# Coarser first loads, a reordered weight product and dummy matmuls at the start of an attention + SwiGLU kernel

## The chip, the cores and the metric

The kernel runs on one core of a Trainium2 chip. The metric is the device time of one execution in microseconds; most executions of one kernel agree within 0.3%. Engines: TensorE (PE, with its weight loads PEld), VectorE (DVE), ScalarE (ACT), GpSimd (POOL), SyncE (SP). L178 is line 178 of the kernel. The chain is the work that ended last, followed back from the last instruction: at each step to what released it. The granted clock is the share of TensorE's full clock that the records of a run show, as a mean over the span unless a time is given. A transfer lands when its completion is signalled.

## The reference, cut to what matters

```python
B, N, C = 4, 6016, 256;  d_ff = 1536;  tau = 1.0
qn = q / (norm(q, axis=1) + 1e-6);  kn = k / (norm(k, axis=1) + 1e-6)
s  = kn.transpose(0, 2, 1) @ qn / tau          # 256 x 256 per batch, summed over 6016 rows
a  = exp(s - s.max(-1));  a /= a.sum(-1) + 1e-9
x  = (v @ a).reshape(B * N, C)
out = (silu(x @ w_gate) * (x @ w_val)) @ w_out
```

The kernel folds the softmax into the weights: once a batch's 256 x 256 matrix is known, it multiplies it with `w_gate` and `w_val`, and the long stream of products with v begins. Batches 2 to 4 are prepared in the background of the one before; only batch 1 has to be read, squared, summed and normalized before anything else can run.

## The kernel before

The parts that the change and the argument touch; "..." marks cuts.

```python
groups = [(s, min(4, NS - s)) for s in range(0, NS, 4)]      # NS = 47 tiles of 128 rows
...
def gemm1_pair(b, t):      # L151, L156: products of q and k, two tiles at a time, into kq
def first_square(b, t, which, on_dve):                       # L165 VectorE, L168 ScalarE
    sq = sqpool.tile([P, 2, C], BF16, tag="sq%d" % which)     # 4 buffers
def first_row_sums(...):   # L178: sums of the squares over rows, by a product with ones
def first_cols / first_col_sums(...):                        # L191, L201: the same per column
...
def keep_warm(n):                                            # L382: results are never read
    ps = psum_o.tile([P, 2, C], FP32, tag="o")
    for _ in range(n):
        nc.tensor.matmul(ps, ones_bf, warm_bf, start=True, stop=True)
...
qgroups = groups[:-1] + [(s, min(2, NS - s)) for s in range(gs, NS, 2)]
order = [(g, 1, groups) for g in range(NG)] + [(g, 0, qgroups) for g in range(NQ)]
for n, (g, which, gl) in enumerate(order):
    load_qk(0, g, which, gl)           # float32 in HBM, fp8 in SBUF, issued by GpSimd
...
load_first_v(); load_w(0, HW); load_w(HW, WP); load_v(*allc[1])
for wc in range(1, NWC):
    load_w(wc * WP, (wc + 1) * WP)
...
for g, which, gl in order:
    ...
    sqs = [first_square(0, t, which, on_dve=(t % 2 == 1)) for t in ts]
    if which == 0:
        for t in ts: gemm1_pair(0, t)
        ...
    for t, sq in zip(ts, sqs):         # row sums of k; row, then column sums of q
        ...
    if which == 0:
        if g == 0: first_norm_k(0); ...
        elif g <= 4: first_inv_k(0, g - 1)      # a quarter of a reciprocal, L218
first_softmax(0)
```

## Time and profile before

| | |
|---|---|
| time, median of 3 | 813.78 us (813.57 to 814.0) |
| profiled span | 811.9 us |
| TensorE busy | 794.1 us |
| last q group landed | 34.07 us |
| first weight product (L392) | 36.53 us |
| TensorE waits for w_gate until | 40.55 us, and never again for long |

The prediction shows the lines and reads them.

### The profile page before, as it was taken

To read this page: it belongs to the slowest core of one execution; us is meant where nothing else is said; L and a number is where in the kernel's file an instruction comes from. 1 tells how busy PE (TensorE), PEld (TensorE's weight loads), DVE (VectorE), ACT (ScalarE), POOL (GpSimd) and SP (SyncE) were. 2 spreads that over 40 slices of the span, in tenths; PEclk is the share of its full clock that TensorE was granted. 3 is DMA by queue.
4 is the path that set the end of the run, shared out by engine and by line. 5 is a ranking of instruction groups with operands and counts; after the bars stand their busy time and mean duration, and the time that the engine had idled before them with its cause. 6 is when DMAs were issued, how large, how long until landed. Compare 5 with 4: busy or idle time off the path is not lost.

```text
span 811.9 us, 13668 instructions
## 1 busy us (share of the span) xinstructions
PE 794.1 (98%) x4952; PEld 488.9 (60%) x5042; DVE 524.3 (65%) x795; ACT 434.8 (54%) x757; POOL 267.2 (33%) x330
## 2 busy tenths in 40 slices
PE   5999999999999999999999999999999999999998
PEld 3656666665565666666565666666556565665666
DVE  4777777657556777656755677765765555555554
ACT  4666655545555556545555556654554544444543
POOL 5515887423000888722100488752300000000000
PEclk9999999999999999999999999999999999999999
DMA  9993875329312678334912377641942112112101
GB/s 87 142 157 69 115 105 86 80 34 150 77 40 46 96 100 106 74 65 95 127 40 59 53 96 112 89 78 37 171 102 66 46 50 55 52 40 65 50 27 59
DMA packets 93747, 64.99 MB, mean 80 GB/s; under 512 B 52896, under 2 KB 92448, under 8 KB 92928
## 3 DMA queue, kind: packets, MB, share of 16 engines
q0 software_dynamic: 19584, 27.41, 29.0%
q1 hardware_dynamic: 73952, 36.65, 18.2%
q8 instruction: 39, 0.64, 0.4%
q14 instruction: 28, 0.23, 0.1%
q10 hardware_dynamic: 144, 0.07, 0.0%
HBM read 79.04 MB, written 36.70 MB: 143 GB/s over the span
## 4 chain that ended last, share of the span: by engine, by line
PE 93%; DMA 4%; issue 1%; DVE 1%; POOL 0%; ACT 0%; POOLq 0%
PE o_new L457 30%; PE v_ps L423 30%; PE g_ps L423 28%; DMA q_sb<-in_q_dram 2%; PE ps L392 2%; PE kq_new L151 2%; DMA k_sb<-in_k_dram 1%; DMA w_gate_sb<-in_moe_w_gate_dram 1%; DVE sv L433 0%; POOL k_sb L106 0%; ACT silu L429 0%; PE last_ps L481 0%; POOL vb L114 0%; DVE sq L274 0%; PE kq_new L156 0%
## 5 line engine op out<-in xcount | busy, mean ns | idle before, releaser
L433 DVE TENSOR_TENSOR sv<-silu,v_ps 128x512 bf16<-128x512 bf16 (+1 forms) x576 | 388.3, 674 | 263.9 <-ACT silu L429 261.1
L429 ACT ACTIVATE silu<-g_ps 128x512 bf16<-128x512 f32 (+1 forms) x576 | 338.7, 588 | 323.4 <-PE g_ps L423 257.5
L457 PE MATMUL o_new<-w_out_sb,sv 128*128 128x256 bf16 x2244 | 337.2, 273 | 1.5
L423 PE MATMUL v_ps<-vT,Wv 128*128 128x512 bf16 (+1 forms) x1100 | 324.3, 374 | 2.9
L423 PE MATMUL g_ps<-vT,Wg 128*128 128x512 bf16 (+1 forms) x1074 | 319.1, 375 | 0.3
L457 PEld LDWEIGHTS <-sv 128*128 128x128 bf16 x2244 | 219.6, 98 | 140.6
L423 PEld LDWEIGHTS <-Wv 128*128 128x128 bf16 x1152 | 112.7, 98 | 130.7
L284 POOL TENSOR_TENSOR acc_new<-acc_new,sq 128x512 f32<-128x512 f32 x135 | 157.6, 1167 | 45.1 <-DVE sq L274 36.9
L423 PEld LDWEIGHTS <-Wg 128*128 128x128 bf16 x1152 | 109.7, 98 | 24.9
L274 DVE TENSOR_TENSOR sq<-q_sb 128x512 bf16<-128x512 fp8e5 x72 | 65.9, 915 | 0.0
L279 POOL TENSOR_TENSOR acc_new<-sq 128x512 f32<-128x512 bf16 x3 | 3.5, 1154 | 150.5 <-DVE sq L274 150.5
L275 ACT ACTIVATE sq<-k_sb 128x512 bf16<-128x512 fp8e5 x72 | 44.2, 614 | 0.0
L466 ACT COPY o_sb<-o_new 128x512 f32<-128x512 f32 x48 | 28.1, 586 | 14.9 <-PE o_new L457 14.5
L151 PE MATMUL kq_new<-k_sb,q_sb 128*128 128x512 fp8e5 x184 | 32.0, 295 | 0.5 <-DMA q_sb<-in_q_dram 0.5
L106 POOL DMA_DIRECT2D q_sb<-in_q_dram x49 | 27.4, 558 | 13.5 <-DMA k_sb<-in_k_dram 5.5
L468 DVE COPY o_sb<-o_new 128x512 f32<-128x512 f32 (+1 forms) x47 | 31.3, 666 | 0.0
L106 POOL DMA_DIRECT2D k_sb<-in_k_dram x48 | 26.0, 542 | 10.4 <-DMA w_out_sb<-in_moe_w_out_dram 5.6
L178 PE MATMUL ss_new<-sq,ones_bf 128*128 128x256 bf16 x83 | 17.8, 353 | 9.1 <-ACT sq L168 8.6
L114 POOL DMA_DIRECT2D vb<-in_v_dram x47 | 24.1, 515 | 5.3 <-DMA vb<-in_v_dram 4.1
L151 PEld LDWEIGHTS <-q_sb 128*128 128x256 fp8e5 x184 | 21.2, 138 | 2.6 <-DMA q_sb<-in_q_dram 2.0
L178 PEld LDWEIGHTS <-ones_bf 128*128 128x128 bf16 x83 | 9.9, 122 | 15.9 <-issue 11.6
L312 POOL TENSOR_TENSOR inv<-inv,half 128x4 f32<-128x4 f32 x3 | 3.1, 1036 | 36.7 <-DVE inv L311 36.7
(94 smaller groups left out, 195.9 us busy)
## 6 DMA issues: line engine op xcount, KB each, us to landing
out_dram<-o_sb SPq DMA_DIRECT2D x92, 256.0 KB, 2.5
vb<-in_v_dram POOLq DMA_DIRECT2D x43, 256.0 KB, 5.9
k_sb<-in_k_dram POOLq DMA_DIRECT2D x44, 128.0 KB, 5.9
q_sb<-in_q_dram POOLq DMA_DIRECT2D x44, 128.0 KB, 5.1
w_out_sb<-in_moe_w_out_dram POOLq DMA_DIRECT2D x1, 768.0 KB, 13.7
vb<-in_v_dram POOLq DMA_DIRECT2D x4, 192.0 KB, 3.5
vT<-vb SPq DMA_TRANSPOSE x47, 4.3
w_gate_sb<-in_moe_w_gate_dram POOLq DMA_DIRECT2D x2, 256.0 KB, 7.0
```

Source lines behind the costliest of these rows:

```text
L106: nc.gpsimd.dma_start(out=dst[:, gs:gs + gm, :], in_=src[b].rearrange("(p s) c -> p s c", s=NS)[:, gs:gs + gm, :])
L151: nc.tensor.matmul(kq[:, jh, :], q_sb[:, ps:ps + 2, js], k_sb[:, ps:ps + 2, :], start=(t == 0 and jh == 0), stop=last, perf_mode=DR, skip_ ...
L178: nc.tensor.matmul(state[b, "ss", which], ones_bf, sq[:, s, :], start=(t == 0 and s == 0), stop=(t == t_last and s == pm - 1))
L274: nc.vector.tensor_mul(sq[:, :pm, 0, :], q_sb[:, ps:ps + pm, :], q_sb[:, ps:ps + pm, :])
L275: nc.scalar.activation(sq[:, :pm, 1, :], k_sb[:, ps:ps + pm, :], ACT.Square)
L284: nc.gpsimd.tensor_tensor(out=acc, in0=acc, in1=sq[:, s, :, :], op=ALU.add)
L423: nc.tensor.matmul(dst[:, :mv], W[:, kk, fs], vT[:, kk, :mv], start=(kk == 0), stop=(kk == CH - 1))
L429: nc.scalar.activation(silu[:, :mv], g_ps[:, :mv], ACT.Silu)
L433: nc.vector.tensor_mul(sv[:, f, :mv], silu[:, :mv], v_ps[:, :mv])
L457: nc.tensor.matmul(self.o_ps[:, j % 2, :], self.sv[:, f, j * P:(j + 1) * P], w_out_sb[:, f, :], start=(f == 0), stop=(f == FH - 1))
L466: nc.scalar.copy(o_sb[:, :m, :], self.o_ps[:, :m, :])
L468: nc.vector.tensor_copy(o_sb[:, :m, :], self.o_ps[:, :m, :])
```

## The change

Its intent: fewer and larger transfers for batch 1's k and q (16 tiles each, then 8, 4, 2 and 1 for q, so that little is left to do after the last landing); a third weight product that needs only the first half of the exponentials; and dummy matmuls that keep TensorE busy while q is awaited. The diff, cut:

```diff
-        sq = sqpool.tile([P, 2, C], BF16, tag="sq%d" % which)
+        sq = sqpool.tile([P, 2, C], BF16, tag="sq%d" % which, bufs=8)
...
+        keep_warm(1)
         transpose_first_v()
-        keep_warm(3)
+        keep_warm(2)
...
         wp_matmul(b, 1, 0, units[1], lo)
+        wp_matmul(b, 2, 0, units[2], lo)
         row_sum(1)
         finish_rs(b, rs)
-        wp_matmul(b, 0, 1, units[0], lo)
-        wp_matmul(b, 1, 1, units[1], lo)
-        for u in (2, 3):
-            for jh in range(CH):
-                wp_matmul(b, u, jh, units[u], lo)
+        for u, jh in ((0, 1), (1, 1), (2, 1), (3, 0), (3, 1)):
+            wp_matmul(b, u, jh, units[u], lo)
...
+    kgroups = [(s, min(16, NS - s)) for s in range(0, NS, 16)]
+    qgroups, at = [], 0
+    while at < NS:
+        rest = NS - at
+        size = 16 if rest >= 39 else 8 if rest >= 23 else 4 if rest >= 4 else min(2, rest)
+        qgroups.append((at, size))
+        at += size
...
-            elif g <= 4:
-                first_inv_k(0, g - 1)
+            elif g <= 2:
+                first_inv_k(0, 2 * g - 2)
+                first_inv_k(0, 2 * g - 1)
+
+            if g < NQ - 2:
+                keep_warm(2)
```

In the changed kernel the dummies are L381, the weight products L391, the products with v L422.

## The prediction

> **What bounds the kernel now.** I read four views in this order: the page, the chain that ended last, the waits, and the timeline of the first 45 us. The page says that nearly the whole span is TensorE work; the chain says so too.
>
> ```profile
> span 811.9 us, 13668 instructions
> PE 93%; DMA 4%; issue 1%; DVE 1%; POOL 0%; ACT 0%; POOLq 0%
> ```
>
> The change touches only the first batch's start, so what it can be worth is read from the chain's early pieces (start, length, what):
>
> ```profile
> 22.93 10.19 DMA q_sb<-in_q_dram
> 33.12 0.28 issue
> 33.40 0.53 POOL vb L114
> 33.93 0.10 issue
> 34.03 6.52 DMA w_gate_sb<-in_moe_w_gate_dram
> 40.55 0.04 issue
> 40.60 1.04 PE ps L392 x4
> ```
>
> Up to 40.55 us the chain is one saturated stream of transfers (k, q, the first v, the weights); from 40.60 us TensorE runs without a gap to the end. So the time is 40.6 us of start plus some 771 us that this change leaves alone, and the change can win or lose only in how soon TensorE reaches that L392 product. The timeline tells what TensorE did before it (start, duration, engine, line, shapes; idle before in brackets):
>
> ```profile
> 7.36 1.01 PE L178 MATMUL ss_new<-sq,ones_bf 128*128 128x256 bf16 x4 [0.19 <-ACT sq L168]
> ...
> 24.74 0.60 PE L178 MATMUL ss_new<-sq,ones_bf 128*128 128x256 bf16 x4
> ...
> 25.24 0.65 PE L151 MATMUL kq_new<-k_sb,q_sb 128*128 128x512 fp8e5 x4
> 25.30 0.63 ACT L168 ACTIVATE sq<-q_sb 128x512 bf16<-128x512 fp8e5 x1 [0.61 <-DMA q_sb<-in_q_dram]
> 25.32 0.69 DVE L165 TENSOR_TENSOR sq<-q_sb 128x512 bf16<-128x512 fp8e5 x1
> ...
> 25.93 0.54 DVE L218 RECIPROCAL ink<-ink 128x64 f32<-128x64 f32 x1
> ...
> 34.82 0.38 PE L356 MATMUL rs<-eps,ones_f 1*128 1x2 f32 x2
> ...
> 36.53 0.38 PE L392 MATMUL unit_ps<-w_gate_sb,exT 128*128 128x256 bf16 x2
> ...
> 39.62 0.59 PE L423 MATMUL v_ps<-vT_new,Wv 128*128 128x512 bf16 x2
> 40.59 0.55 PEld L392 LDWEIGHTS <-exT 128*128 128x128 bf16 x4 [0.87 <-DMA w_gate_sb<-in_moe_w_gate_dram]
> ```
>
> The reader is to see three things. All engines keep pace with the loads: each group of four tiles is worked off as it lands, so that only about 0.8 us lies between the last q landing (34.07 us) and L356. From 36.53 us TensorE goes on without a pause until the issue of v_ps ends at about 40.05 us, then waits 0.55 us for the weights: that 0.55 us is all the room its own chain has. And the same four row-sum matmuls took 1.01 us at 7.36 us and 0.60 us at 24.74 us: start to start 213 ns then, 108 ns later, the step falling near 21.6 us.
>
> **What the Trainium skill says.** "DMA: Bandwidth & Descriptors", section "Why small descriptors are slow (HBM only)", gives a fixed cost of about 3 cycles per packet beside its 32-byte beats; with the 850 MHz of its section "Where 436 GB/s comes from", a 4096-byte read is (128+3)/0.85 = 154 ns. The trace agrees: the squares of the k groups start 1.25 us apart, and one engine moves 8 such packets a group, 1.233 us, which leaves 0.021 us for the completion. The packet records say that size is linear: 173 ns for 4096 source bytes, 98 for 2048, 60 for 1024, and 1226 for the 32768 of a v transfer, that is 37.65 ns per KB plus 22 ns, of which all but about 3.5 overlaps the next packet. "Perfetto Trace Analysis", section "DMA Optimizations", says that larger transfers amortize a per-transfer overhead but that splitting lets some work start sooner; this change trades the second for the first. "TensorE: Matmul & The Clock Gate", Part 1, says that the array runs at half rate until about 3.4 us of sustained work; the 213 and 108 ns agree, although the page's clock row shows 9 throughout.
>
> **The change part by part.**
>
> *Fewer transfers.* Per engine, k and q are now 25 transfers of 8 packets (200 packets, 25 completions); after, 3 + 8 = 11 transfers (88 packets, 11 completions). Saved: 112 x 3.5 ns + 14 x 21 ns = 0.69 us. Sixteen tiles take 8 x (16 x 37.65 + 3.5) + 21 ns = 4.87 us, fifteen 4.57, eight 2.46, four 1.25, two 0.65, one 0.35. The fourth k group landed at 9.22 us; less 24 packets and 3 completions (0.15) the first large one lands at 9.07, the next at 13.94 and 18.51, then q: 23.38 (16 tiles), 25.84, 28.30, 29.55, 30.80, 32.05, 32.70, 33.05. The stream is the same bytes at the same rate, so the large q group lands 3.2 us after the first small one did (20.18).
>
> *What the grouping moves.* No q work can begin before 23.4 us. From there TensorE works in program order: all products of a group, its row sums (column sums from the fifth group), two dummies of 0.216 us each for the first six groups. With the fast spacing, 0.109 us a product and 0.108 a row sum:
> - group 1: 23.4 + 16 x 0.109 = 25.14; 16 row sums 26.87; dummies 27.30.
> - group 2: 8 products 28.17. Its squares on VectorE come late: ScalarE has four squares and the two steps of ink first (23.4 + 4 x 0.63 + 0.79 = 26.71), VectorE the ink addition and a cast (27.2), two squares 28.60. Row sums 28.88, dummies 29.31. VectorE's two reciprocals (0.54 each): 29.68.
> - group 3: products 30.18; VectorE squares at 31.06; row sums 31.34; dummies 31.77; reciprocals 32.14.
> - group 4: products 32.21; square 32.83; row sums 33.11; dummies 33.54.
> - group 5: VectorE copies the row (0.41) at 33.33 and is at 33.74; the row's transposition on TensorE (0.54) ends at 34.52, column sums 34.74, dummies 35.17.
> - group 6: products 35.61, column sums 35.83, dummies 36.26.
> - groups 7 and 8: products 36.73, column sums 36.92; L356 is done at 37.17, against 35.07 now.
>
> The check on this sum: TensorE's q work after 23.4 us is 48 x 0.109 + 36 x 0.108 + 0.54 + about 0.6 for column sums = 10.3 us, plus 12 dummies x 0.216 = 2.6 us: 36.3 us even without one wait. VectorE alone has 11 x 0.69 + 0.42 + 0.5 + 4 x 0.54 + 0.41 = 11.1 us: 34.5 us.
>
> *The softmax.* Now the first exponentials end 1.48 us after the last column sum (34.755 to 36.23). After: 36.92 + 1.48 = 38.40, first weight product about 38.50 + 0.05. The dummy before the transposes fills a wait for v that is gone by then (v lands near 34.3); TensorE's own list would be through at 38.3, so it costs nothing.
>
> *The third product.* It puts one 0.108 us matmul ahead of the second row sum, which now starts at 36.75 with no gap before it; after, it fills part of the 0.45 us between the two exponentials. Worth 0 to 0.1 us; I leave a stall of 0.1 us.
>
> *Sum.* First weight product 38.55 + 0.10 against 36.53: 2.1 us later. Of this 0.55 us is the room before the weights; they land earlier themselves, so TensorE no longer waits for them. 2.1 - 0.55 = 1.55 us. 813.78 + 1.55 = 815.3 us.
>
> **Rivals.**
> 1. The transfers stay the bound. Then the whole start moves with them: -0.7 us, 813.1. For it: at present everything after 12 us waits on landings, and bigger packets may also help in the ragged first microsecond, where some packets took up to 1.08 us. Against it: even at zero overhead the large q group can't land much before 22.5 us, and the 13 us of TensorE work behind it then pass 35.4.
> 2. TensorE is slow when the large q group lands. TensorE idles for about 1 us before it. If it stays slow until 26.8 or 28.4 us (one or two windows of the size that the skill gives), the same addition ends 1.0 to 1.9 us later: 816.4 to 817.2. Against it: in bursts of sixteen row sums at 213 ns (3.4 us without pause of every 4.9 us) it has a better chance to warm up during k than now, where 0.85 us of every 1.25 never did. I go by warm.
> 3. The dummies do no harm, because TensorE waits for VectorE anyway. Taking them out of my addition moves the first weight product about 1 us earlier, not 2.6, so VectorE's backlog is the other half; 814.3 would be the result if they hid completely.
>
> **Range and chances.** All of this is a fraction of 1% of the span: nothing in 40 us of start can lose or gain the 16 us that 2% asks for. Rival 1 bounds the low side with rival 3 inside, rival 2 the high side. I take 813.9 to 817.2, with about one chance in ten that it comes out faster than now. Chances: faster by over 2% 0.005, within 2% 0.985, slower by over 2% 0.01.
>
> **What would show the steps right or wrong.** Landings: ScalarE's squares of k should resume near 9.1, 13.9 and 18.5 us, and of q near 23.4; if q's come before 22.5, the saving per packet is larger than I think. In the waits, q's squares should no longer be ended by the transfer from group 2 on, but run back to back on VectorE. L356 near 36.9 and the first L392 near 38.6; TensorE should not wait for w_gate at all, and the chain should run through L178, L151, VectorE's squares and the dummies' line in place of the transfer of w_gate. If L356 comes before 35 us, the backlog was misjudged and rival 1 holds; if the row sums after 23.4 us are 213 ns apart, rival 2 does.

## The result, and the profile after

| | before | after |
|---|---|---|
| time, median of 6 runs each | 813.83 us (813.57 to 814.0) | 815.17 us (814.92 to 815.57) |
| profiled span | 811.9 us | 813.2 us |
| w_gate's second columns landed | 40.55 us | 39.90 us |
| first weight product | 36.53 us | 38.26 us |
| first product with those columns | 40.60 us | 41.80 us |

The ratio is 1.0017 (95% interval 1.0004 to 1.003): 1.3 us slower. Ratios here are the mean time of one kernel's runs over that of the other's of the same rounds, so not quite the ratio of the medians.

The page of the changed kernel, the lines that answer to those of before:

```profile
span 813.2 us, 13666 instructions
PE 95%; DMA 2%; issue 1%; DVE 0%; ACT 0%; POOL 0%; POOLq 0%
```

DMA's share of the chain is halved. The chain itself (start, length, what) shows where it went:

```profile
3.59 19.71 DMA q_sb<-in_q_dram
23.31 0.04 issue
23.35 1.96 PE kq_new L151 x16
25.31 1.76 PE ss_new L178 x16
...
29.27 0.43 PE ps L381 x2
29.70 0.87 PE kq_new L151 x8
30.57 0.89 PE ss_new L178 x8
31.46 0.43 PE ps L381 x2
...
36.46 0.14 PE cols L201 x6
...
37.63 0.52 ACT exT L241
...
38.40 0.35 PE unit_ps L391 x3
```

The transfer now ends at 23.31 us, with the large q group. From 23.35 to 36.60 us the chain is TensorE, piece after piece, with the dummies of L381 between the groups; VectorE's squares are not in it. In the timeline (start, duration, engine, line, shapes; idle before in brackets) VectorE waits for TensorE, TensorE waits for the exponential with the moved dummy already done, and the product that used to wait for w_gate waits for nothing:

```profile
32.82 0.41 DVE L183 COPY row<-ss_new 1x256 f32<-1x256 f32 x1 [1.48 <-PE ss_new L178]
...
36.34 1.06 POOL L553 DMA_DIRECT2D w_out_sb<-in_moe_w_out_dram  x1
36.49 0.42 DVE L225 TENSOR_TENSOR s_f<-kq_new,ink 128x256 f32<-128x256 f32 x1 [1.73 <-PE kq_new L156]
...
37.06 0.34 DVE L226 TENSOR_SCALAR inq<-inq 128x2 f32<-128x2 f32 x1
...
38.19 0.11 PEld L247 LDWEIGHTS <-exT 128*128 128x128 bf16 x2 [0.59 <-ACT exT L241]
...
41.80 1.03 PE L391 MATMUL ps<-w_gate_sb,exT 128*128 128x512 bf16 x4
```

So the transfers delivered what they promised (w_gate 0.65 us sooner) and TensorE no longer keeps up with them: its first weight product is 1.73 us later, its room before w_gate was 0.55 us, and 1.73 - 0.55 = 1.18 us is what the first product with the second columns shows (41.80 against 40.60: 1.20 us). The dummy that was moved in front of the transposes had no run of its own; the 0.59 us that TensorE still waits after it say that it cost nothing here.

### The profile page after: what moved, and what is told of

The parts are those of the page before. It is cut to its first block, busy times and chain, and to the rows that moved or that the text cites. A ratio compares the mean times of both kernels' runs of the same rounds, so it can differ in the third digit from the quotient of the medians.

```text
span 813.2 us, 13666 instructions
## 1 busy us (share of the span) xinstructions
PE 790.9 (97%) x4962; PEld 489.2 (60%) x5054; DVE 522.2 (64%) x795; ACT 433.3 (53%) x757; POOL 260.8 (32%) x316
## 4 chain that ended last, share of the span: by engine, by line
PE 95%; DMA 2%; issue 1%; DVE 0%; ACT 0%; POOL 0%; POOLq 0%
PE o_new L456 31%; PE v_ps L422 30%; PE g_ps L422 29%; PE kq_new L151 3%; DMA q_sb<-in_q_dram 2%; PE ps L391 2%; PE ss_new L178 0%; PE ps L381 0%; DVE sv L432 0%; ACT silu L428 0%; PE last_ps L480 0%; POOL k_sb L106 0%; PE kq_new L156 0%; PE unit_ps L391 0%; PE cols L201 0%
## 5 line engine op out<-in xcount | busy, mean ns | idle before, releaser
L422 PE MATMUL v_ps<-vT,Wv 128*128 128x512 bf16 (+1 forms) x1100 | 324.3, 374 | 2.8
L422 PE MATMUL g_ps<-vT,Wg 128*128 128x512 bf16 (+1 forms) x1074 | 319.0, 375 | 0.3
L422 PEld LDWEIGHTS <-Wv 128*128 128x128 bf16 x1152 | 112.7, 98 | 130.8 <-ACT Wv L403 0.2
L422 PEld LDWEIGHTS <-Wg 128*128 128x128 bf16 x1152 | 109.6, 98 | 24.8
L106 POOL DMA_DIRECT2D q_sb<-in_q_dram x44 | 24.8, 566 | 14.0 <-DMA k_sb<-in_k_dram 11.3
L178 PE MATMUL ss_new<-sq,ones_bf 128*128 128x256 bf16 x83 | 13.4, 320 | 13.7 <-ACT sq L168 13.7
L106 POOL DMA_DIRECT2D k_sb<-in_k_dram x39 | 21.2, 543 | 11.9 <-DMA w_out_sb<-in_moe_w_out_dram 5.8
```

Of the source, the lines that this page charges most:

```text
L106: nc.gpsimd.dma_start(out=dst[:, gs:gs + gm, :], in_=src[b].rearrange("(p s) c -> p s c", s=NS)[:, gs:gs + gm, :])
L422: nc.tensor.matmul(dst[:, :mv], W[:, kk, fs], vT[:, kk, :mv], start=(kk == 0), stop=(kk == CH - 1))
```

## The experiments

Theory A: TensorE's own list from the large q group on is the new bound, and the dummies are the part of it that buys nothing. Rivals: VectorE's backlog is half of it; the dummies are needed for the clock; the grouping or the reordered products lose by themselves. The runs came in four sets: each set compares its kernels with the kernel before on the same chip.

### Without the dummies in the q loop

```diff
-            if g < NQ - 2:
-                keep_warm(2)
```

> The changed kernel without the dummies inside the q loop (12 of them, 2.6 us of TensorE issue). Theory A, TensorE's own list after the large q group is the bound (in the changed kernel it runs from 23.35 to 36.6 us without a pause): without the dummies TensorE catches up with the landings near 31.5 us, the last column sum comes near 34.0 us, the first weight product near 35.8, and TensorE waits for w_gate again, which lands at 39.9 us instead of 40.55. So 0.65 us faster than the kernel before: about 813.2 us, 2.0 us under the changed one. Theory B, VectorE's backlog is the other half (the prediction's third rival): only about 1 us under the changed one, 814.2 us. Theory C, the dummies are needed to keep TensorE at the fast spacing: products 0.213 us apart in places and about 815 us or more.

Measured: 813.04, 813.12 and 813.17 us in three runs, 814.21 and 814.45 us in two; the kernel before in the same rounds 813.82 us (813.53 to 814.39). The profiled run is the 813.04. Its chain:

```profile
33.37 6.60 DMA w_gate_sb<-in_moe_w_gate_dram
39.97 0.05 issue
40.01 1.04 PE ps L391 x4
```

w_gate is back as the bound, 0.58 us sooner than before (39.97 against 40.55), and the time follows (the median of the five is 0.65 us under that of the kernel before). In the three lower runs that is theory A to 0.2 us: about 2 us come back, not the 1 us of the VectorE theory. But the two upper runs were foreseen by no theory, and over all five the ratio is 0.9996 (0.9983 to 1.0009): the same as before.

### Twice as many dummies

`keep_warm(4)` in place of `keep_warm(2)` in the q loop.

> The changed kernel with four dummies a group in place of two, 12 more of 0.216 us. Theory A (TensorE's list is the bound from the large q group on): every one is paid in full, 2.6 us more than the changed kernel, about 817.8 us. If some wait of another engine or a landing hides a part of them: less than 2.0 us more.

Measured: 817.5 us in the profiled run, 819.04 to 819.41 us in four more; before 813.82 us. By the profiled spans, no, two and four dummies a group give 811.3, 813.2 and 815.7 us. The ratio of all five is 1.0061 (1.0049 to 1.0074). The second dozen costs 2.5 us of its 2.6: nothing hides it. The first dozen costs 1.9, because without it TensorE waits again: 0.45 us for w_gate, and a few tenths for a landing and for VectorE near 31 and 32 us. Again there is an upper group.

### The third product alone, and the dummies alone

The kernel before with the reordered products:

> The kernel before with the reordered weight products alone. Both theories: no difference that can be told, 813.6 to 814.0 us, because TensorE there has no pause around the second row sum and waits 0.55 us for w_gate afterwards in any case. If the reorder were the cause of the loss, it would be 1 us slower.

Measured 813.88 us (813.71 to 814.78), before 813.82: ratio 1.0001 (0.9989 to 1.0014). The reorder is worth nothing that can be seen. The kernel before with two dummies after each of its first eleven q groups:

```diff
             elif g <= 4:
                 first_inv_k(0, g - 1)
+            if g < NQ - 2:
+                keep_warm(2)
```

> The kernel before with two dummies after each of its first eleven q groups of four tiles. Per group TensorE then has 0.87 + 0.43 = 1.30 us of work against a landing every 1.254 us, and begins them at the slow spacing, so a backlog builds up: the last column sum near 36.8 us instead of 34.75, 2.0 us later, less the 0.55 us of room before w_gate: about 815.3 us. That would say that the dummies alone make up the whole loss and the grouping none of it. If the coarse grouping is what loses, it stays within 0.5 us of the kernel before.

Measured 814.87 us (814.15 to 815.81), before 813.82: ratio 1.0011 (0.9998 to 1.0025), 1.05 us, so two thirds of the 1.5 expected, and the interval just reaches 1. The profiled run, at 815.81 us the slowest of the five, shows how the backlog builds up (chain):

```profile
21.47 0.88 PE ss_new L178 x4
22.35 0.22 issue
22.57 0.63 PE ps L382
23.21 0.85 PE kq_new L151 x4
...
24.58 0.43 PE ps L382 x2
25.01 0.44 PE kq_new L151 x4
25.45 0.45 PE ss_new L178 x4
```

At the full clock a group takes 0.43 + 0.44 + 0.45 = 1.32 us against a landing every 1.25, which adds only 0.07 us a group. Most of this run's backlog is older: TensorE came to its first full-clock record at 24.07 us, so its first groups went at half speed (0.85 and 0.88 us for the same pieces). The third group had landed at 22.78 us and began at 25.01, 2.2 us late; the tenth, landed at 32.00, began at 34.25, as late. So dummies can lose with fine groups too, here mainly because they leave no time to make up for a slow clock; how the four faster runs split was not traced.

### The two groups of times

The changed kernel once more, with the other kernels of its set, on another chip:

> The changed kernel once more, on the chip of the following three. In the last set the kernel without dummies had two groups of times (813.04 to 813.17 and 814.21 to 814.45 us), and the one with four dummies too (817.5 and 819.04 to 819.41). Theory S: these are runs in which TensorE is still at its slow spacing (213 ns) when the large q group lands, and stays so for a while (the prediction's second rival, as chance by run). Then the changed kernel too should show a second group 1 to 2 us above 815.2 in some of its runs. If it never does, in 5 runs and the 6 of the first set, the two groups come from something else, such as that chip.

Measured: 815.14 us once and 816.34, 816.36, 816.62 and 816.77 us; before 813.71 us (813.55 to 814.18); ratio 1.0034 (1.0021 to 1.0048). So the changed kernel has the upper group too; the six runs of the first set simply had none of it. The runs' mean granted clock parts them: 1.0 for the first, 0.996 for each of the four. The kernel before is not free of such runs, but has few: 3 of its 35 took 814.39, 814.56 and 814.68 us, at 0.996 to 0.998, and the reordered products' slowest (814.78) reads 0.996. The kernel without dummies, again:

> The kernel without dummies once more. Theory S: again two groups, near 813.1 and 814.3 us, and every run of the upper one with a clock of 0.996 or less, every run of the lower with 0.998 or more.

Measured 813.11 and 813.26 us at a clock of 1.0 and 0.998; 814.4, 814.58 and 815.14 us at 0.996, 0.996 and 0.995; before 813.79 us. This time the profiled run is of the upper group. The table of windows (busy us and count for PE, PEld, DVE, ACT, POOL, then granted clock, DMA share and GB/s), first the lower run, then the upper one:

```profile
23.20:26.60 3.40, 3.21 (x29) 3.00 (x30) 2.79 (x6) 3.20 (x7) 1.06 (x2) 1.00 1.06 107
```

```profile
23.20:26.60 3.40, 2.85 (x14) 2.85 (x15) 2.50 (x4) 2.84 (x6) 0.69 (x2) 0.50 1.07 108
```

TensorE does 14 matmuls at half clock where it did 29. In the chain of the upper run the sixteen products take twice as long:

```profile
23.75 3.68 PE kq_new L151 x16
27.43 1.85 PE ss_new L178 x16
```

The first group is through in 5.5 us instead of 3.5. The changed kernel was lucky only at the last moment in its own trace: its windows show 0.64 for 18.40 to 23.20 us, with a full clock again from 22.65 us on.

```profile
18.40:23.20 4.80, 3.33 (x15) 2.01 (x14) 2.23 (x4) 2.19 (x4) 0.53 (x1) 0.64 0.99 102
```

To force it, the changed kernel without the row sums of the second and third k group (a wrong k norm):

```diff
             else:
-                first_row_sums(0, t, which, sq, (T_COLS if which == 0 else NP) - 1)
+            elif which == 0:
+                first_row_sums(0, t, which, sq, T_COLS - 1)
+            elif g == 0:
+                first_row_sums(0, t, which, sq, 7)
```

(The edit also replaces the bare `else`.)

> Wrong result on purpose: the changed kernel without the row sums of the second and third k group, so that TensorE idles from about 13 us to the large q group at 23.4 us and must be at its slow spacing then. The clock records of the traces so far change only in steps of 3.41 us, and the runs of the upper groups (816.34 to 816.77 us of the changed kernel, 814.21 and 814.45 of the one without dummies) have a mean granted clock of 0.995 or 0.996, those of the lower 0.998 to 1.0. Theory S: q's products begin 213 ns apart and stay so for 3.4 to 6.8 us, which costs 1.2 to 3 us more: 816.4 to 818.2 us in all runs, none near 815.2. If it comes out at 815.2, the slow spacing is not what parts the groups.

Measured 816.53, 816.9, 817.24 and 817.37 us, before 813.79: all in the upper range, none near 815.2. In the trace q's sixteen products stand 213 ns apart, and the chain has them as in the upper run above:

```profile
23.35 3.67 PE kq_new L151 x16
27.02 1.80 PE ss_new L178 x16
```

With that run this shows the slow clock at the large q group as a cause of the right size. No trace of an upper run of the changed kernel itself was kept, so that its four are the same is inferred from their times and clocks. Two things to know: the output comparison does not see a k norm that leaves out two thirds of the rows; and two of these runs read a mean clock of 1.0. The kernel before reads 1.0 too, though its row sums run 213 ns apart until its first clock record at 21.65 us, so time ahead of the first record seems to be counted as full speed; the profiled lower run without dummies holds no clock record at all and reads 1.0 as well. Nor does the mean clock part the groups everywhere; of the runs with four dummies the lower one (817.5 us) reads 0.997, and one upper one (819.04 us) 0.998. The spacing of equal matmuls is the surer sign.

### The same dummies where TensorE has nothing to do

```diff
-            if g < NQ - 2:
-                keep_warm(2)
+        else:
+            keep_warm(3)          # after each k group
```

> The changed kernel with its dummies moved: none after the q groups, three after each of the three k groups, where TensorE idled for 1.4 to 1.8 us. Theory A (dummies cost what TensorE's list has no room for): these cost nothing, the time is that of the run without dummies, 813.2 us. Theory S: TensorE is then busy without a pause from 14.6 us on and surely at the fast spacing at 23.4 us, so that all runs fall in one group, within 0.4 us. If two groups 1 us apart remain, theory S is wrong.

Measured 813.24 us (813.17, 813.18, 813.24, 813.48 and 814.02), clock 1.0 in all five; before 813.71 us. No second group at 814.3, though the five are not as close as expected. The ratio is 0.9996 (0.9984 to 1.0009): 0.47 us by the medians, which five runs can't tell from nothing. Its trace has no clock record, but each pair of its row sums stands 108 ns apart from 19.7 us on. Of the versions it is the one with low times and no clear second group; none was faster than the kernel before by more than the noise.

### Large groups for k alone

The kernel before with `kgroups` and 8 buffers; q in fours, no dummies.

> The kernel before with k alone in groups of 16, 16 and 15; q in its old groups of four, no dummies in the loop. Saved in the stream: 72 packets of 3.5 ns and 9 completions of 21 ns, 0.44 us, and no large q group at all. Theory A: q's work starts at about 19.7 us and keeps pace, so w_gate lands 0.44 us sooner and the time is 813.4 us. If coarse loads lose something of their own (squares of k late, TensorE's last k row sums in the way of q), it is 813.8 us or more.

Measured 813.55 us (813.2 to 813.7), before 813.71: ratio 0.9997 (0.9984 to 1.0009). No loss from coarse loads as such, and no upper group although the clock was 0.998 in two runs. That q in fours lets TensorE start early enough to make up for a slow clock is a guess; no slow run of this kernel was traced. The gain is within the noise and under the 0.44 us of the transfers: in the trace w_gate lands at 40.25 us but TensorE's own list reaches it only at 40.37, so the list is the bound there.

### Two tries at the v load

The kernel with the dummies in k, with the second v chunk's load moved behind the second pair of weight columns, and behind their gate half alone:

> A try to beat both: as the run with the dummies in k, and the second v chunk is loaded after the second pair of weight columns instead of before it. The run without dummies waits for w_gate (0.45 us) until 39.97 us; with the v load of 1.25 us behind it, w_gate lands near 38.7 us and TensorE's own list, through at 39.57 us, is the bound: 0.4 us less, about 812.7 us. Against it: the second chunk's transposes then start 2.6 us later and landed at about 49 us before; chunk two begins near 51.7 us, and if they come later than that the gain is lost.

> A milder try at the v load: as the run with the dummies in k, with the second v chunk's load between the second gate and the second value columns. The gate columns then land near 38.7 us, before TensorE gets to them at 39.57 us; the value columns near 41.2 us, needed at 41.3. 812.8 us, if the transposes of that chunk, which now start 1.3 us later (near 40 us), land before 51.7 us; they took 9 to 10.7 us in the kernels before and after and 15.4 us when they started at 41.1 us beside w_out.

Measured 820.09 to 822.7 us in four runs (before 813.71), and 813.28 to 813.77 us in three runs with 816.88 to 817.34 us in three others (before 813.79). The risk that the expectations name is what happened. The chain of the second one's profiled run:

```profile
40.34 13.87 DMA vT<-vb
```

TensorE stood until 54.21 us for the transposes of that chunk. In the first it was 15.44 us, until 56.57. Neither is a gain.

## Why the prediction was right or wrong, point by point

- **Transfers** (right). Saved: 0.69 us predicted, 0.65 us measured at w_gate. Single traces scatter: the second columns landed at 40.55 to 40.85 us in the three with all the old loads, at 39.78 to 40.16 in the seven with all the new ones. The prediction's 154 ns a packet, and the 3.5 ns of it that larger packets save, are an estimate from the skill's figures; no run here measures the 3.5 ns alone. The large groups' squares began at 9.02, 13.93, 18.49 and 23.33 us; landings were predicted for 9.07, 13.94, 18.51 and 23.38. The fifth q group landed at 31.46 us, not 30.80, and the rest 0.3 to 0.4 us late, which TensorE's backlog hid.
- **TensorE's list as the new bound** (right, and shown by the runs with no, two and four dummies). The last column sum was predicted for 36.92 us and ends at 36.60 in the chain. The terms that were mis-sized are VectorE's, 0.69 us a square and 0.54 a reciprocal, where back to back it took 0.62 (2.50 for four) and 0.48, and ScalarE's 0.63 a square, where it took 0.55 (2.19 for four), so that VectorE's second group could start at 26.61 us. VectorE held up none of the row sums of groups 2 to 4 and is not in the chain, where the prediction had put its squares. Its sign for the waits came true for VectorE alone: ScalarE's squares were still ended by transfers (1.41 us at 31.56). The plain sum of TensorE's list in the prediction, 36.3 us, missed by as much as the schedule with its waits, on the other side.
- **The third rival's reason against itself** (wrong). "VectorE's backlog is the other half" does not hold: without dummies the lower runs gained about 2 us, not 1.
- **The softmax** (mis-sized). 1.48 us were carried over from the last column sum to the end of the first exponential. Counted in both traces from the last column sum's start, it is 1.55 us before (34.73 to 36.28) and 1.72 after (36.42 to 38.14). The 0.17 us is L226, which took 0.34 us instead of 0.17. It ended at 37.40 us, together with GpSimd's issue of w_out (36.34 + 1.06). In the upper run of the kernel without dummies it took 0.73 us and ended at 37.61, again with that issue (36.55 + 1.07). The other two traces in which it took longer (0.33 and 0.34 us) also have it end within 0.03 us of a GpSimd issue that began before it; in one of them that issue is of a weight load, not of w_out. In the nine others it took 0.17. The Trainium skill, "SBUF — State Buffer", section "Who interferes with whom", says that a VectorE `tensor_scalar` can need the port pair it shares with GpSimd and then blocks until GpSimd's instruction is done. The lines agree; no run was made to test it.
- **The sum.** 2.1 us later predicted, 1.73 measured; room 0.55 both; total 1.55 predicted, 1.34 measured. VectorE and ScalarE were taken for slower than they are and the softmax for quicker, and the errors partly cancel. That the first median came within 0.13 us of 815.3 also owes something to luck: in the second set of the same kernel it was 816.36.
- **The third product** (right): nothing to be seen.
- **The second rival** (wrongly weighed). "I go by warm" described the six runs of the first set and one of the five of the second. The other four are what the second rival gave, 816.4 to 817.2 us: they came out at 816.34 to 816.77. It is not a rival but a second outcome of the same kernel, and how often it comes can't be said from none of six and four of five. The two ends that the prediction gave its slow stretch, 26.8 and 28.4 us, are not counted from one start (23.4 and 21.6 us); where it was traced it lasted until 27.49 and 26.98 us.
- **"About one chance in ten that it comes out faster"**: none of eleven runs did; all eleven lie in the range.

## What to carry to other kernels

Before a large transfer replaces small ones, add up what the slowest consumer must still do after it lands: here the stream gained 0.65 us, and TensorE, which had been fed in steps, got 13 us of work at once with no time left to do it in. A dummy matmul is free only where the engine would have idled to the next wait; put it in front of the wait that keeps the engine idle, not behind each piece of work. When a kernel's times fall in two groups, look at each run's granted clock and at the spacing of equal matmuls before comparing medians.

## What the Trainium skill lacked or had wrong

- "TensorE: Matmul & The Clock Gate", Part 1: it lets the array go slow after an idle window and fast after a busy one, and gives no share of work for either. Here 0.85 us of row sums in every 1.25 us (68%) never released it, in 12 us of the kernel before. In the changed kernel a window with 2.7 of 3.41 us of work (9.00 to 12.41 us, 79%) did. And the slow clock came back at 19.23 us after a window (15.82 to 19.23) that was not idle: seven row sums began in it, about 0.8 us at 108 ns each. The windows are taken to end at the clock records, which stand 3.41 us or whole multiples of it apart.
- "DMA: Bandwidth & Descriptors", section "DMA Transpose (X-bar)": it gives no time for a transpose beside other queued loads. The same chunk's transposes took 9.1 us from issue to landing in the kernel before (39.33 to 48.41 us), and 13.87 and 15.44 us in the runs that issued them 1.0 and 1.8 us later. The w_out load was queued beside them in all three, so it does not explain the difference, which stays open.
